# Half of the attention weights transposed by DMA as float16 pairs instead of by TensorE, and two feed-forward stages exchanged

## The chip, the cores and the metric

One core of one Trainium2 chip. The metric is the device time of one execution in microseconds, the median of the runs shown. Float32 in, float32 out.

## The reference

Three computations in a row. Sizes: batch 2, 8 heads, 576 positions, head width 64, so 1152 tokens of 512 features.

```python
scores = (q @ k.T) / 8                          # 576 x 576 per batch and head
kth    = the 32nd largest score of each row
attn   = softmax over the scores >= kth; all other weights 0
x = (attn @ v), heads side by side              # 1152 x 512
h = x @ w_in                                    # 512 -> 2048
y = (max(h, 0) + alpha * min(h, 0)) @ w_out     # 2048 -> 512
out = ((y @ w_a) * (y @ w_b)) @ w2              # 512 -> 1536 -> 512
```

## The kernel before

**Tiles and groups.** Attention is cut into 72 tiles: 128 query rows of one head (kind `T`), or 64 rows of two heads (kind `L`, the last 64 positions). `M1` (L46) sorts the tiles into six groups of output tokens, which the two feed-forward layers then take as their columns. Groups 0 and 1 are 128 tokens of batch 0 (8 tiles each), group 2 is 256 tokens of batch 0 (16 tiles), group 3 is 256 tokens: the last 64 of batch 0, the last 64 and the first 128 of batch 1 (16 tiles), group 4 is 256 tokens of batch 1 (16 tiles), group 5 is 128 tokens of batch 1 (8 tiles).

**One attention tile.** `front` (L406): TensorE makes the scores, ScalarE copies them to SBUF. `middle` (L419): VectorE finds the 32 largest of each row with four MAX8 and three MATCH_REPLACE8 (L424 to L433), ScalarE takes the exponential (L437), VectorE masks it and sums (L440), GpSimd scales the rows (L444). `back` (L450), for the tile before: TensorE turns the 128 x 576 weights round in five float32 transposes (L458, L460), ScalarE copies the two PSUM tiles to the tile `pt` (L459, L461). `av` (L466), after the last tile of a unit (one `L` tile, two heads of one `T` tile, or two heads of two neighbouring `T` tiles): ten float32 matmuls (twenty instructions, in two column halves of TensorE, L481) multiply with `v`; ScalarE and VectorE write the result to `xT` as a float16 high and low part (L488, L489). `fetch_v` loads `v` again for each group and head pair (28 loads).

**The feed-forward layers.** `moe1(g)` and `moe2(g)` are the first and second layer for the tokens of group g. From group 2 on both run in float16 pairs: each value is a high and a low part and three matmuls stand for one (`contract` L550, `project` L562). The high part is a cast on ScalarE (L540), the low part a subtraction on GpSimd (L541). `finish` (L615) turns the result of `moe1` round for `moe2`: a square with its sum (L620), power-of-two scales on VectorE (L109 to L111), two casts (L630, L631), eight transposes (L635), a copy (L636).

**What sets the order.** `ORDER` (L48) lists the stages: (1, 4) is `moe1` of group 4. Three tracks are interleaved by a planner's clocks (L739 to L867): `dve_track` (conversion of the weights, then attention, 6.1 planned us a tile, given out in ninths, `STEPS`), `mlp_track` (the stages), `bg_track` (weights rewritten as float16 pairs). A stage `moe1(g)` waits until the attention of group g is planned to be done. The framework then gives every engine a fixed order of its own, in which it runs without overtaking. All loads and the stores of rewritten weights are issued by SP, in one order too: `q` and `k` (L328, L347), `v` (L339), the weight blocks of the last layer (L246, L251, L672). Outputs go out from ScalarE's queue.

Of the kernel before, what the change touches and what calls it, by code (L numbers as in the profile page):

```python
# [8 lines left out]
F32 = mybir.dt.float32  # L9
F32R = mybir.dt.float32r  # L10
F16 = mybir.dt.float16
# [5 lines left out]
AF = mybir.ActivationFunctionType  # L17
ALU = mybir.AluOpType

P = 128  # L20
B, H, S, D = 2, 8, 576, 64
# [6 lines left out]
HALF = S // 2  # L28
NEG = -3.0e38

NORM = "pool"
RLOB = 3
W2B = 3
# [2 lines left out]
VB = 2  # L36
# [4 lines left out]
PB = 3  # L41
# [6 lines left out]
ORDER = ((1, 0), (2, 0), (1, 1), (2, 1), (1, 2), (2, 2), (1, 3), (2, 3), (1, 4), (1, 5), (2, 4), (2, 5))  # L48
# [14 lines left out]
KBACK = 2  # L63
# [17 lines left out]
def tile_topk_attention_moe(ctx: ExitStack, tc: tile.TileContext, qT, kT, vM, vL, wi, wo, al, wa, wb, w2, out):  # L81
    nc = tc.nc
    cp = ctx.enter_context(tc.tile_pool(name="cp", bufs=1))
    sp = ctx.enter_context(tc.tile_pool(name="sp", bufs=2))
# [48 lines left out]
    vsc = small("vsc", 2)  # L133
# [181 lines left out]
    late = []  # L315
# [6 lines left out]
    qcur, xts = {}, {}  # L322
    kcur, vcur = {}, {}
# [43 lines left out]
    for g, grp in enumerate(M1):  # L367
        cols_of = {}
        col = 0
        for kind, b, t in grp:  # L370
            cols_of[kind, b, t] = col
            col += P if kind == "T" else D
        for hp in range(4):

            units = []
            for kind, b, t in grp:
                if units and len(units[-1]) < 2 and kind == "T" and units[-1][0][:2] == (kind, b):
                    units[-1].append((kind, b, t))
                else:
                    units.append([(kind, b, t)])  # L380
            for unit in units:
                pts_of = {}
                for slot, (kind, b, t) in enumerate(unit):
                    n = P if kind == "T" else D
                    heads = [[2 * hp], [2 * hp + 1]] if kind == "T" else [[2 * hp, 2 * hp + 1]]
                    for i, hs in enumerate(heads):
                        tiles.append(dict(g=g, b=b, t=t if kind == "T" else 4, hp=hp, hs=hs, n=n, col=cols_of[unit[0]], slot=slot,
                                          wide=len(unit) * P, pts=pts_of, last=slot == len(unit) - 1 and i == len(heads) - 1))
        gsize.append(col)

    def fetch(tl):
        b, t, hp = tl["b"], tl["t"], tl["hp"]
        tl["k"] = {h: get_k(b, h) for h in tl["hs"]}
        if (b, t, hp) not in qcur:
            qcur[b, t, hp] = prep_q(b, t, hp)

    def fetch_v(tl):
        b, t, hp = tl["b"], tl["t"], tl["hp"]
        if (tl["g"], b, hp) not in vcur:
# [19 lines left out]
    def middle(tl, s):  # L419
        m8 = sp.tile([P, 32], F32, tag="m8", name="m8", bufs=3)  # L420
        nb = sp.tile([P, 1], F32, tag="nb", name="nb", bufs=2)
        e = sp.tile([P, S], F32, tag="e", name="e", bufs=EB)
        wk = sp.tile([P, S], F32, tag="wk", name="wk", bufs=WKB)
        nc.vector.max(m8[:, 0:8], s)  # L424
        nc.gpsimd.tensor_scalar(nb, m8[:, 0:1], -0.125, None, op0=ALU.mult)
        yield 1
        src = s
        w2 = lambda t: t.rearrange("p (a n) -> p a n", a=2)
        ep = None
        for r in range(1, 4):  # L430
# [10 lines left out]
        nc.vector.tensor_scalar(sm[:, 1:2], sm[:, 0:1], 1e-9, None, op0=ALU.add)  # L441
# [5 lines left out]
        tl["e"] = e  # L447
        yield 1

    def back(tl):  # L450
        e = tl["e"]
        j = tl["hs"][0] % 2
        if tl["slot"] == 0:
            tl["pts"][j] = sp.tile([P, 5, 2 * P], F32, tag="pt", name="pt", bufs=PB)
        pt = tl["pts"][j][:, :, tl["slot"] * P:tl["slot"] * P + P]
# [10 lines left out]
    def av(pair_):  # L466
        tl = pair_[-1]
        g, hp, n, col = tl["g"], tl["hp"], tl["n"], tl["col"]
        v = vcur[g, tl["b"], hp]
        if g not in xts:  # L470
            if split_in[g] or gsize[g] > P:
                xts[g] = late[0].tile([P, 4, 256], F32, tag="xT", name=f"xT{g}", bufs=XB)
            else:
                xts[g] = sp.tile([P, 4, P], F32, tag="xe", name=f"xe{g}", bufs=2)
        o = psum("o", "T")
        wd = tl["wide"]
        for c in range(5):
            for j in range(2):
                pt = tl["pts"][j if n == P else 0]
                pt = pt[:, c, 0:wd] if n == P else pt[:, c, j * D:(j + 1) * D]  # L480
                nc.tensor.matmul(o[j * D:(j + 1) * D, 0:n if n == D else wd], v[:, c, j * D:(j + 1) * D], pt, start=c == 0, stop=c == 4)  # L481
        if n == P:
            n = wd
        for r, c in [(slice(0, P), slice(0, n))]:
            if split_in[g]:
                x = split_view(xts[g])
                xh = x[r, 0, hp, col:col + n]
                nc.scalar.activation(xh, o[r, c], AF.Copy, scale=vsc[r, 0:1])  # L488
                nc.vector.scalar_tensor_tensor(x[r, 1, hp, col:col + n], o[r, c], vsc[r, 0:1], xh, op0=ALU.mult, op1=ALU.subtract)  # L489
            else:  # L490
                nc.scalar.activation(xts[g][r, hp, col:col + n], o[r, c], AF.Copy)

    def attention():
        for tl in tiles[0:F0]:
            fetch(tl)
        ready = [front(tiles[0])]
        yield ("begin", 0)
        for tl in tiles[F0:FA]:
            fetch(tl)
        ready += [front(tl) for tl in tiles[1:QA]]  # L500
        for tl in tiles[0:VA]:
            fetch_v(tl)
        prev = None
        pr = []
        for i, tl in enumerate(tiles):
            s = ready.pop(0)
            for k, _ in enumerate(middle(tl, s)):
                if k == 0 and i + FA < len(tiles):
                    fetch(tiles[i + FA])
                if k == 1 and i + VA < len(tiles):  # L510
                    fetch_v(tiles[i + VA])
                if k == KBACK and prev is not None:
                    back(prev)
                    pr.append(prev)
                    if prev["last"]:
                        av(pr)
                        pr = []
                    yield ("done", prev["g"])
# [6 lines left out]
        av(pr)  # L525
        yield ("done", prev["g"])


    def wide(tag, bufs):
# [226 lines left out]
    def dve_track():  # L756
        att = attention()
        cnt = [0] * len(M1)
# [10 lines left out]
        def advance():  # L769
            r = next(att, None)  # L770
            if isinstance(r, tuple):
                cnt[r[1]] += 1
                if cnt[r[1]] == need[r[1]]:
                    att_done[r[1]] = clock["dve"] + 3
                return 1
            return r and 0

        for kind, k, *more in DVE:
# [5 lines left out]
            if kind == "mix":  # L784

                done, steps = 0, 0
# [16 lines left out]
            else:  # L803
                left = k
                while left:
                    r = advance()
# [103 lines left out]
```

## Time and profile before

| what | us |
|---|---|
| three runs | 724.32, 725.1, 728.9 |
| median | 725.1 |
| profiled execution | 727.69 |
| its span, first to last instruction | 725.9 |
| TensorE busy in the span | 634.6 (87%) |
| VectorE | 570.8 (79%) |
| ScalarE | 471.4 (65%) |
| GpSimd | 377.3 (52%) |

The profiled execution lies 2.6 us above the median, and 1.8 us of it lie outside the span. Times in the rows below count from the span's first instruction. PE is TensorE, PEld its weight loads, DVE VectorE, ACT ScalarE, POOL GpSimd, SPq the issuing queue of SP. A matmul's listed duration is longer than the distance to the next one, since matmuls are pipelined.

### The profile page before, as it was taken

The page shows a single profiled execution, that of the slowest core. Times are in us where ns is not written, and L with a number is a line of the kernel's source. Part 1 is how long each engine was busy: PE and PEld are TensorE (multiplying, and loading weights), DVE is VectorE, ACT ScalarE, POOL GpSimd, SP SyncE. Part 2 cuts the span into 40 slices and gives each one's busy share as a digit, 9 for nine tenths or more (in the row PEclk, how much of TensorE's full clock was granted, in tenths as well). Part 3 has the DMA queues.
Part 4 walks back from the last instruction along what each step waited for, and adds up shares of the span by engine and source line. Part 5 has one row for each costly group of instructions (what it writes and reads, how often), then busy time and mean ns, then how long its engine had stood idle before and what let it go on. Part 6 is the DMA issues. An engine that isn't in the chain of part 4 may idle for free.

```text
span 725.9 us, 14586 instructions
## 1 busy us (share of the span) xinstructions
PE 634.6 (87%) x5002; PEld 473.2 (65%) x5002; DVE 570.8 (79%) x1462; ACT 471.4 (65%) x995; POOL 377.3 (52%) x540
## 2 busy tenths in 40 slices
PE   1456866999979889799869999999999999999997
PEld 1334655687756658567637877766777777677775
DVE  3999899789989998998579799999889899322121
ACT  4878987896789877888676544556445455543222
POOL 5776788886655666879564422433223233221111
PEclk9975569999999999899989999999999999999999
DMA  6976999994411133212545134010122300002243
GB/s 176 326 248 198 352 290 288 311 339 130 133 43 28 26 93 87 76 52 85 163 142 156 54 83 121 28 32 22 26 67 80 98 17 17 2 2 59 61 129 102
DMA packets 60410, 86.15 MB, mean 119 GB/s; under 512 B 7984, under 2 KB 34608, under 8 KB 60336
## 3 DMA queue, kind: packets, MB, share of 16 engines
q1 hardware_dynamic: 59024, 82.87, 36.7%
q10 hardware_dynamic: 1312, 2.36, 0.9%
q8 instruction: 39, 0.64, 0.4%
q14 instruction: 35, 0.29, 0.1%
HBM read 76.55 MB, written 8.65 MB: 117 GB/s over the span
## 4 chain that ended last, share of the span: by engine, by line
PE 47%; DVE 3%; ACT 3%; DMA 2%; issue 2%; POOL 1%; POOLq 0%; ACTq 0%; DVEq 0%
PE h L550 8%; PE y L562 8%; PE ha L550 8%; PE hb L550 8%; PE o L562 7%; PE o L481 3%; PE ps L413 3%; DMA w2s<-w_st 2%; PE t L458 2%; DVE m L433 1%; DVE wk L431 1%; ACT xT L636 1%; PE t L460 0%; ACT wsc L248 0%; DVE e L440 0%
## 5 line engine op out<-in xcount | busy, mean ns | idle before, releaser
L433 DVE MAX8 m<-wk 128x8 f32<-128x576 f32 x216 | 162.8, 754 | 2.0
L541 POOL TENSOR_TENSOR gp<-gt,gp 128x256 f16<-128x256 f32 (+1 forms) x112 | 68.2, 610 | 150.9 <-ACT gp L540 141.6
L431 DVE MATCH_REPLACE8 wk<-m,wk 128x576 f32<-128x576 f32 x144 | 106.8, 742 | 0.0
L550 PE MATMUL h<-xT,wi_sb 128*128 128x256 f16 (+1 forms) x960 | 100.1, 251 | 5.1 <-DVE gp_n L599 4.0
L550 PEld LDWEIGHTS <-wi_sb 128*128 128x128 f16 x960 | 79.1, 98 | 27.1 <-issue 11.0
L540 ACT ACTIVATE gp<-gt 128x256 f16<-128x256 f32 (+1 forms) x112 | 43.4, 388 | 74.6 <-DVE gt L690 52.6
L562 PEld LDWEIGHTS <-gp 128*128 128x128 f16 x588 | 54.9, 98 | 47.0 <-ACT gp L540 1.9
L562 PE MATMUL y<-wo_sb,gp 128*128 128x512 f16 x336 | 84.1, 379 | 0.6 <-ACT gp L540 0.4
L444 POOL TENSOR_SCALAR e<-e,sm 128x576 f32<-128x576 f32 x72 | 55.1, 765 | 51.0 <-DVE sm L442 44.5
L413 PE MATMUL ps<-ks,qh 128*128 128x288 f32 x160 | 49.9, 390 | 32.2 <-DVE e L440 23.1
L424 DVE MAX8 m<-s 128x8 f32<-128x576 f32 x72 | 54.2, 753 | 26.7 <-ACT s L416 25.1
L690 DVE SCALAR_TENSOR_TENSOR gt<-hb,wb_inv,r 128x256 f32<-128x256 f32 (+1 forms) x48 | 21.4, 446 | 61.2 <-PE hb L550 59.7
L550 PE MATMUL ha<-xT,wa_sb 128*128 128x256 f16 (+1 forms) x576 | 65.7, 262 | 1.6 <-ACT xT L636 1.6
L550 PE MATMUL hb<-xT,wb_sb 128*128 128x256 f16 (+1 forms) x576 | 64.3, 260 | 0.0
L562 PE MATMUL o<-w2s,gp 128*128 128x512 f16 x252 | 63.6, 380 | 0.4 <-ACT gp L540 0.2
L481 PE MATMUL o<-pt,v 128*64 128x128 f32 (+2 forms) x640 | 56.8, 319 | 5.4 <-ACT pt L459 2.3
L550 PEld LDWEIGHTS <-wa_sb 128*128 128x128 f16 x576 | 51.1, 99 | 15.6 <-issue 2.6
L440 DVE SCALAR_TENSOR_TENSOR e<-s,m,ep 128x576 f32<-128x576 f32 x72 | 58.0, 806 | 2.3 <-ACT ep L437 0.2
L413 PEld LDWEIGHTS ps<-ks,qh 128*128 128x128 f32 x160 | 29.1, 214 | 43.9 <-issue 14.9
L190 ACT ACTIVATE rlo<-raw 128x512 int16<-128x512 uint32 x68 | 53.8, 791 | 5.7 <-DMA raw<-in_wi_dram 3.9
L458 PE MATMUL t<-ident,e 128*128 128x128 f32 x288 | 48.1, 293 | 10.5 <-POOL e L444 10.3
L437 ACT ACTIVATE ep<-s,nb 128x576 f32<-128x576 f32 x72 | 53.7, 745 | 3.0 <-POOL ql L353 0.6
(192 smaller groups left out, 1411.6 us busy)
## 6 DMA issues: line engine op xcount, KB each, us to landing
w2s<-w_pr SPq DMA_DIRECT2D x48, 256.0 KB, 2.6
w2s<-w_st SPq DMA_DIRECT2D x36, 256.0 KB, 2.7
raw<-in_wi_dram SPq DMA_DIRECT2D x16, 512.0 KB, 6.3
raw<-in_wo_dram SPq DMA_DIRECT2D x16, 512.0 KB, 6.7
v<-in_vM_dram SPq DMA_DIRECT2D x28, 256.0 KB, 3.2
raw<-in_wa_dram SPq DMA_DIRECT2D x12, 512.0 KB, 5.3
raw<-in_wb_dram SPq DMA_DIRECT2D x12, 512.0 KB, 5.1
raw<-in_w_dram SPq DMA_DIRECT2D x12, 512.0 KB, 5.4
```

The costliest lines, as they stand in the source:

```text
L190: nc.scalar.activation(r.bitcast(I16).rearrange("p (n t) -> p n t", t=2)[:, :, 0], lo, AF.Copy, scale=2.0 ** -29)
L413: nc.tensor.matmul(ps[:, f, 0:HALF], q[:, h % 2, :], ks[h][:, f * HALF:(f + 1) * HALF], start=i == 0, stop=i == len(mm) - 1)
L424: nc.vector.max(m8[:, 0:8], s)
L431: nc.vector.match_replace(out=wk, in_to_replace=m8[:, 8 * r - 8:8 * r], in_values=src, imm_value=NEG)
L433: nc.vector.max(m8[:, 8 * r:8 * r + 8], wk)
L440: nc.vector.scalar_tensor_tensor(w2(e), w2(s), m8[:, 31:32], ep, op0=ALU.is_ge, op1=ALU.mult, accum_out=sm[:, 0:1])
L444: nc.gpsimd.tensor_scalar(e, e, sm[:, 1:2], 1.0, op0=ALU.mult, op1=ALU.mult)
L458: nc.tensor.transpose(t1[:, c * P:(c + 1) * P], e[:, c * P:(c + 1) * P], ident)
L481: nc.tensor.matmul(o[j * D:(j + 1) * D, 0:n if n == D else wd], v[:, c, j * D:(j + 1) * D], pt, start=c == 0, stop=c == 4)
L541: nc.gpsimd.tensor_sub(l[:, 0:n], t[:, 0:n], h[:, 0:n])
L550: nc.tensor.matmul(dst[:, 0:n], w[a][:, c * P:(c + 1) * P], x[:, b, c, 0:n], start=k == 0, stop=k == 11)
L562: nc.tensor.matmul(dst, act[b][:, s], w[a], start=i == 0 and k == 0, stop=i == last and k == 2)
```

## The change

For tiles of batch 1 (the second half, tiles 36 to 71) `back` no longer uses TensorE. The scaled weights, times 2^14, are cast to float16 on ScalarE, the remainder is made by two subtractions on GpSimd, both halves stand side by side in `e16` (128 x 1152, one buffer), and one transposing DMA from SP writes nine 128 x 128 blocks into `pt`. `v` of batch 1 is loaded once per head pair, at tiles 20, 26, 38 and 40, and kept as a float16 pair (`v_pair`). `av` multiplies high by high, low by high and high by low: 28 float16 matmuls instead of 20 float32 instructions, and it stands one tile later (`KAV`). In group 3 the four `L` tiles of batch 0 come first. In `ORDER`, `moe2` of group 4 comes ahead of `moe1` of group 5. A "done" step now covers a whole unit instead of a tile, so a tile takes between 8.25 and 8.5 planner steps instead of nine. The tile `xe` has one buffer instead of two.

```diff
-ORDER = (..., (1, 4), (1, 5), (2, 4), (2, 5))
+ORDER = (..., (1, 4), (2, 4), (1, 5), (2, 5))
+KLIFT = 3
+KAV = 1
+KV = 4
+V_AT = {20: 0, 26: 1, 38: 2, 40: 3}
...
+    def v_pair(hp):
...
+        raw = flat(sp.tile([P, 5, 2 * P], F32, tag="pt", name="vraw", bufs=PB))...
+        nc.sync.dma_start(raw[:, 0:4, :], vM[1, :, :, c0:c0 + 2 * D])
+        for r in (slice(0, D), slice(D, P)):
+            nc.sync.dma_start(raw[r, 4, :], vL[1, :, c0:c0 + 2 * D])
+        vh, vl = pr[:, 0:5], pr[:, 5:10]
+        nc.scalar.activation(flat(raw), flat(raw), AF.Copy, scale=vsc[:, 0:1])
+        nc.scalar.activation(flat(vh), flat(raw), AF.Copy)
+        nc.gpsimd.tensor_sub(flat(vl), flat(raw), flat(vh))
+        nc.gpsimd.memset(vl[D:P, 4], 0.0)
...
+        if tl["lift"]:      # in middle, after the scaling on GpSimd
+            e16 = late[0].tile([P, 2 * S], F16, tag="e16", name="e16", bufs=1)
+            nc.scalar.activation(e16[:, 0:S], e, AF.Copy)
+            nc.gpsimd.tensor_sub(e16[:, S:S + D], e[:, 512:S], e16[:, 512:S])
+            nc.gpsimd.tensor_sub(e16[:, S + D:2 * S], e[:, 0:512], e16[:, 0:512])
...
+        if tl["lift"]:      # in back
+            pt = lifted(tl["pts"][j])[:, :, tl["slot"] * P:tl["slot"] * P + P]
+            nc.sync.dma_start_transpose(pt, e)
+            return
...
+        if lift:            # in av
+            ops = [(vh, c, c) for c in range(5)] + [(vh, c, 5 + c) for c in range(4)] + [(vl, c, c) for c in range(5)]
+            for i, (w, a, c) in enumerate(ops):
+                for j in range(2):
...
+                    nc.tensor.matmul(o[j * D:(j + 1) * D, ...], w[:, a, j * D:(j + 1) * D], pt, start=i == 0, stop=i == 13)
...
+                if k == KV and i in V_AT:
+                    v_pair(V_AT[i])
+                if k == KAV and due:
+                    p = due.pop(0)
+                    av(p)
+                    yield ("done", p[0]["g"], len(p))
```

## Rows read from the trace of the kernel before

**Rows 1.** The page: busy tenths of the engines in 40 equal slices.

```profile
PE   1456866999979889799869999999999999999997
...
DVE  3999899789989998998579799999889899322121
```

**Rows 2.** Stretches: us, busy (instructions) of PE, PEld, DVE, ACT, POOL; clock, DMA share, GB/s.

```profile
293.00:387.00 94.00, 77.45 (x576) 54.46 (x574) 74.95 (x186) 74.02 (x151) 67.77 (x103) 0.91 0.36 110
...
511.00:572.00 61.00, 61.00 (x468) 46.59 (x468) 53.96 (x126) 28.34 (x61) 18.31 (x33) 0.97 0.22 63
572.00:626.00 54.00, 54.00 (x429) 38.93 (x427) 44.76 (x109) 27.62 (x64) 18.54 (x33) 1.00 0.11 32
626.00:726.00 100.00, 94.96 (x950) 71.67 (x948) 22.56 (x62) 35.42 (x93) 19.98 (x40) 1.00 0.22 64
```

**Rows 3.** VectorE alone: stretch, us, busy (instructions), clock, DMA share, GB/s.

```profile
387.00:557.00 170.00, 155.83 (x374) 0.99 0.21 62
557.00:615.00 58.00, 55.25 (x131) 1.00 0.16 47
```

**Rows 4.** VectorE's groups between 437 and 557 us (one masking instruction per tile).

```profile
L440 DVE SCALAR_TENSOR_TENSOR e<-s,m,ep 128x576 f32<-128x576 f32 x16 | 13.0, 810 | 1.0
```

**Rows 5.** The chain that ended last, pieces of it: start us, us, what.

```profile
565.39 2.31 PE o L481 x20
...
578.46 0.44 PE t L458 x4
578.89 0.11 PE t L460
...
579.65 1.31 PE h L550 x12
...
581.39 1.24 PE o L481 x20
...
702.76 0.67 PE ha L550 x12
```

**Rows 6.** Groups of ScalarE and GpSimd: busy us, mean ns, idle before.

```profile
L459 ACT ACTIVATE pt<-t 128x512 f32<-128x512 f32 x72 | 42.8, 595 | 18.0 <-PE t L458 17.4
L461 ACT ACTIVATE pt<-t 128x128 f32<-128x128 f32 x72 | 20.0, 277 | 3.2 <-PE t L460 3.2
L250 POOL TENSOR_TENSOR w2s<-wsc,w2s 128x512 f16<-128x512 f32 x12 | 13.9, 1158 | 11.4 <-ACT w2s L249 8.7 <-issue 1.8 <-POOL w2s L250 0.8
L331 ACT ACTIVATE ks<-kr 128x576 fp32r<-128x576 f32 x16 | 10.8, 676 | 3.3 <-DMA kr<-in_kT_dram 2.0 <-PE ps L413 1.3
L361 POOL TENSOR_TENSOR ql<-qr,qh 128x64 fp32r<-128x64 f32 x16 | 4.8, 321 | 0.0
```

**Rows 7.** DMA issues: KB each, median us from issue to landing.

```profile
w2s<-w_pr SPq DMA_DIRECT2D x48, 256.0 KB, 2.6
...
raw<-in_wo_dram SPq DMA_DIRECT2D x16, 512.0 KB, 6.7
...
qr<-in_qT_dram SPq DMA_DIRECT2D x64, 64.0 KB, 2.3
...
alpha<-in_al_dram SPq DMA_DIRECT2D x1, 8.0 KB, 1.6
```

**Rows 8.** What SP's queue waited for: us in total, times, longest.

```profile
SPq L672 <- PE o L562: 166.8, 43, 59.3
...
SPq L339 <- PE o L481: 50.0, 12, 15.1
```

**Rows 9.** Timeline at the end of `moe1` of groups 3 and 5.

```profile
501.99 1.46 PE L562 MATMUL y<-wo_sb,gp 128*128 128x512 f16 x6
...
510.99 1.22 PE L550 MATMUL ha<-xT,wa_sb 128*128 128x256 f16 x5 [1.58 <-ACT xT L636]
...
652.05 0.59 PE L562 MATMUL y<-wo_sb,gp 128*128 128x512 f16 x2
...
657.85 1.02 ACT L636 ACTIVATE xT<-tp 128x1024 f16<-128x1024 f16 x1
```

More of the change, by code (lines that the diff above doesn't have):

```diff
@@ L29 @@
 NEG = -3.0e38
+LIFT = 2.0 ** 14
+KLIFT = 3
+KAV = 1
+KV = 4
+V_AT = {20: 0, 26: 1, 38: 2, 40: 3}
 NORM = "pool"
@@ L46 @@
 M1 = [[('T', 0, 0)], [('T', 0, 1)], [('T', 0, 2), ('T', 0, 3)], [('L', 0, 0), ('L', 1, 0), ('T', 1, 0)], [('T', 1, 1), ('T', 1, 2)], [('T', 1, 3)]]
[L48 removed]
+ORDER = ((1, 0), (2, 0), (1, 1), (2, 1), (1, 2), (2, 2), (1, 3), (2, 3), (1, 4), (2, 4), (1, 5), (2, 5))
 PAIRS = ("wi", "wo", "wa", "wb", "w2")
@@ L372, in tile_topk_attention_moe @@
             col += P if kind == "T" else D
-        for hp in range(4):
+        lead = grp[0][0] == "L" and len(grp) > 1
+        for part, hp in [(p, h) for p in ((grp[:1], grp[1:]) if lead else (grp,)) for h in range(4)]:
             units = []
-            for kind, b, t in grp:
+            for kind, b, t in part:
                 if units and len(units[-1]) < 2 and kind == "T" and units[-1][0][:2] == (kind, b):
@@ L387, in tile_topk_attention_moe @@
                         tiles.append(dict(g=g, b=b, t=t if kind == "T" else 4, hp=hp, hs=hs, n=n, col=cols_of[unit[0]], slot=slot,
-                                          wide=len(unit) * P, pts=pts_of, last=slot == len(unit) - 1 and i == len(heads) - 1))
+                                          wide=len(unit) * P, pts=pts_of, lift=b == 1, last=slot == len(unit) - 1 and i == len(heads) - 1))
         gsize.append(col)
@@ L395, in fetch @@
             qcur[b, t, hp] = prep_q(b, t, hp)
+    vpair = {}
+    def v_pair(hp):
+        c0 = hp * 2 * D
+        flat = lambda t: t.rearrange("p c n -> p (c n)")
+        if hp < 2:
+            pr = late[0].tile([P, 5, 2 * D], F32, tag="vp", name=f"vp{hp}", bufs=2)
+        else:
+            pr = sp.tile([P, 5, 2 * D], F32, tag="v", name=f"vp{hp}", bufs=VB)
+        pr = flat(pr).bitcast(F16).rearrange("p (c n) -> p c n", c=10)
+        raw = flat(sp.tile([P, 5, 2 * P], F32, tag="pt", name="vraw", bufs=PB))[:, 0:5 * P].rearrange("p (c n) -> p c n", c=5)
+        nc.sync.dma_start(raw[:, 0:4, :], vM[1, :, :, c0:c0 + 2 * D])
[6 more added lines that the diff above has]
+        nc.gpsimd.memset(vl[D:P, 4], 0.0)
+        vpair[hp] = vh, vl
     def fetch_v(tl):
         b, t, hp = tl["b"], tl["t"], tl["hp"]
-        if (tl["g"], b, hp) not in vcur:
+        if not tl["lift"] and (tl["g"], b, hp) not in vcur:
             v = sp.tile([P, 5, 2 * D], F32, tag="v", name=f"v{b}{t}{hp}", bufs=VB)
@@ L440, in middle @@
         nc.vector.scalar_tensor_tensor(w2(e), w2(s), m8[:, 31:32], ep, op0=ALU.is_ge, op1=ALU.mult, accum_out=sm[:, 0:1])
-        nc.vector.tensor_scalar(sm[:, 1:2], sm[:, 0:1], 1e-9, None, op0=ALU.add)
+        if tl["lift"]:
+            nc.vector.tensor_scalar(sm[:, 1:2], sm[:, 0:1], 1e-9, 1.0 / LIFT, op0=ALU.add, op1=ALU.mult)
+        else:
+            nc.vector.tensor_scalar(sm[:, 1:2], sm[:, 0:1], 1e-9, None, op0=ALU.add)
         nc.vector.reciprocal(sm[:, 1:2], sm[:, 1:2])
@@ L447, in middle, with lifted @@
         tl["e"] = e
+        if tl["lift"]:
[3 more added lines that the diff above has]
+            nc.gpsimd.tensor_sub(e16[:, S + D:2 * S], e[:, 0:512], e16[:, 0:512])
+            tl["e"] = e16
         yield 1
+    def lifted(t):
+        return t.rearrange("p c n -> p (c n)").bitcast(F16)[:, 0:9 * 2 * P].rearrange("p (c n) -> p c n", c=9)
     def back(tl):
@@ L468, in av @@
         g, hp, n, col = tl["g"], tl["hp"], tl["n"], tl["col"]
-        v = vcur[g, tl["b"], hp]
+        lift = tl["lift"]
+        if lift:
+            vh, vl = vpair[hp]
+        else:
+            v = vcur[g, tl["b"], hp]
         if g not in xts:
@@ L473, in av @@
             else:
-                xts[g] = sp.tile([P, 4, P], F32, tag="xe", name=f"xe{g}", bufs=2)
+                xts[g] = sp.tile([P, 4, P], F32, tag="xe", name=f"xe{g}", bufs=1)
         o = psum("o", "T")
         wd = tl["wide"]
-        for c in range(5):
+        if lift:
+            ops = [(vh, c, c) for c in range(5)] + [(vh, c, 5 + c) for c in range(4)] + [(vl, c, c) for c in range(5)]
+            for i, (w, a, c) in enumerate(ops):
+                for j in range(2):
+                    pt = lifted(tl["pts"][j if n == P else 0])
+                    pt = pt[:, c, 0:wd] if n == P else pt[:, c, j * D:(j + 1) * D]
+                    nc.tensor.matmul(o[j * D:(j + 1) * D, 0:n if n == D else wd], w[:, a, j * D:(j + 1) * D], pt, start=i == 0, stop=i == 13)
+        for c in range(0 if lift else 5):
             for j in range(2):
@@ L503, in attention @@
         prev = None
-        pr = []
+        pr, due = [], []
         for i, tl in enumerate(tiles):
@@ L511, in attention @@
                     fetch_v(tiles[i + VA])
-                if k == KBACK and prev is not None:
+                if k == KV and i in V_AT:
[4 more added lines that the diff above has]
+                    yield ("done", p[0]["g"], len(p))
+                if prev is not None and k == (KLIFT if prev["lift"] else KBACK):
                     back(prev)
                     pr.append(prev)
-                    if prev["last"]:
+                    if prev["last"] and prev["lift"]:
+                        due.append(pr)
+                        pr = []
+                    elif prev["last"]:
                         av(pr)
+                        yield ("done", prev["g"], len(pr))
                         pr = []
-                    yield ("done", prev["g"])
                 if k == KFRONT and i + QA < len(tiles):
@@ L524, in attention @@
         pr.append(prev)
-        av(pr)
-        yield ("done", prev["g"])
+        for p in due + [pr]:
+            av(p)
+            yield ("done", p[0]["g"], len(p))
     def wide(tag, bufs):
@@ L771, in advance @@
             if isinstance(r, tuple):
-                cnt[r[1]] += 1
+                cnt[r[1]] += r[2]
                 if cnt[r[1]] == need[r[1]]:
                     att_done[r[1]] = clock["dve"] + 3
-                return 1
+                return r[2]
             return r and 0
```

6 lines of the change are left out of this document (4 added, 2 removed).

## The prediction

> **What bounds the kernel now.** I read the page's forty slices first [rows 1]. TensorE stands at eight or nine tenths from the sixth slice on, VectorE at the same height up to slice 34, where the last attention tile ends, and at two or three tenths behind it. So two engines are nearly full side by side for most of the kernel, and TensorE alone at its end. The stretches make that exact [rows 2]. From 511 to 572 us (`moe2` of group 3 beside the attention of group 4) TensorE is busy all 61 us; from 572 to 626 (`moe1` of group 4 beside the attention of group 5) all 54 us; from 626 on 95 of 100. Only 293 to 387 us is different: there TensorE leaves 16.5 us and VectorE 19 us of 94 unused, while ScalarE (74) and GpSimd (68) rewrite weights and loads through SP's queue stand between them. VectorE alone [rows 3] is busy 155.8 us of the 170 from 387 to 557, so 14.2 us are idle, and 55.3 of 58 behind that. That decides how a saving on TensorE is to be counted: ahead of 572 us, where `moe1` of group 4 waits for the attention of group 4, it is worth no more than VectorE's idle time; behind 572 us it is worth all of itself.
>
> **TensorE's saving.** In the chain the five transposes of a tile cost 0.44 + 0.11 = 0.55 us [rows 5]. All 36 tiles of batch 1 lose them: 19.8 us. The product with `v` goes from 20 instructions to 28. A float16 matmul of 256 columns costs 1.31 / 12 = 0.109 us, one of 128 columns 0.67 / 12 = 0.056 us [rows 5]. A float32 transpose of 128 columns costs 0.11 us, twice the float16 price; twenty float32 instructions of 256 columns would cost 20 x 0.22 = 4.4 us at that rate, and the row has 2.31 us. So the two column halves run side by side already, and I take the same for the new 14 pairs: 14 x 0.109 = 1.53 us instead of 2.31 for a unit of four tiles (0.8 saved, four units in group 4), 14 x 0.056 = 0.78 instead of 1.24 for a unit of two (0.46 saved, four in group 3, four in group 5). That is 3.1 + 3.7 = 6.8 us. If the halves did not overlap in float16, the units would cost 3.05 and 1.57 us and the product would lose 5.6 us instead; I take the overlapped value and keep the other for the range. Split by stretch: ahead of 572 us 28 x 0.55 + 3.1 + 1.8 = 20.3 us, behind it 8 x 0.55 + 1.8 = 6.2 us.
>
> **Ahead of 572 us.** Of the 20 us only VectorE's gaps can be cashed in: 14.2 us between 387 and 557, and part of the 19 us before 387. VectorE's instructions per tile stay as they were. I count 11 of the 14.2, because some gaps are waits for scores and exponentials from ScalarE that remain, and 2 of the earlier 19, since there the new casts, subtractions and transposes of tiles 36 to 40 and the two late loads of `v` meet the engines and the queue that are busy already. Together 13 us. The bounds are 0 (VectorE keeps its pace) and about 25.
>
> **What the other engines get.** ScalarE loses 0.595 + 0.277 us of copies per tile and gains one cast of 128 x 576, for which a cast of that size in another place has 0.676 us [rows 6]: 0.2 us less. GpSimd gains two subtractions per tile; the nearest rows are 0.321 us (64 columns) and 1.158 us (512 columns) [rows 6], so 1.5 us a tile and 53 us in all. Between 511 and 572 us it is busy 18.3 of 61 us [rows 2], and some eight tiles a stretch add 12: it has room. The four `v` pairs cost by the same rows about 1.5 us on ScalarE and as much on GpSimd each, beside a full TensorE; the 12 loads of `v` that go are off the path, but SP's queue waited 50 us for TensorE to free `v` buffers [rows 8], with loads of `q` and of weights behind it. I cost this at nothing either way.
>
> **The transposing DMA.** The trace has none, so its time to landing, L, is bounded. It moves 288 KB. A 64 KB load lands after 2.3 us, a 256 KB one after 2.6, a 512 KB one, at a busy time, after 6.7 [rows 7]. The nearest is the 256 KB row; scaled it gives 2.9 us, and I take 3.5, since a turned block is not a plain row. What it may cost is set by the single buffer `e16`: the cast for the next tile waits on ScalarE until the DMA has read the last one, and behind that cast stand the next exponential and score copy, for which VectorE waits. One turn of that ring is the cast 0.68, the subtractions 0.32 and 1.16, some 0.7 us queued behind other work of GpSimd (my estimate, one subtraction's order) and L: 2.86 + L. The attention has one tile per 120 / 16 = 7.5 us [rows 4]. So L = 3.5 gives a ring of 6.4 us, hidden; at L = 4.6 us it is as slow as the tiles are now, and each further us of L costs 36 us. On SP the transpose also waits for GpSimd, and loads of `q` and of `w2` queue behind it, for a us or two; the queue itself is mostly waiting for TensorE to free weight buffers (166.8 us [rows 8]), so the loads come ahead of need. For the product with `v` the landing has about one whole tile, which 3.5 us fits. The Trainium skill speaks to L twice, and not with one voice. "VectorE: DVE Perf Modes", section "The three transpose paths", gives the DMA 1309 ns for one 128 x 128 block against 390 ns on TensorE; nine of them one after another would be 11.8 us, and the time by it some 250 us above the time before. "DMA: Bandwidth & Descriptors", section "Latency and other measured facts", gives 261 GB/s for such DMAs, which is 1.1 us of moving for 288 KB, inside what I take. No row here shows either.
>
> **The exchanged stages.** Before, the end of `moe1` of groups 4 and 5 was covered by the start of the next independent stage. Now `moe2` of the same group follows at once and needs the turned result. In group 5's case, from the last matmul (652.05 + 0.59) to the copy's end (657.85 + 1.02) it took 6.2 us [rows 9], then with other work in its way; I count 5 us of idle TensorE for it. In group 4's case the nearest is group 3, 503.45 to 510.99 us [rows 9], 7.5 us in which attention filled most and the last 1.6 us were a plain wait; I count 2. What the exchange buys is that TensorE need not wait for the attention of group 5, which VectorE finishes no sooner than about 64 us after that of group 4 (eight tiles at 7 us and the way through the DMA), while `moe1` of group 4 with a lighter attention takes some 50. That wait does not stand in the time before, so it is a loss avoided and no gain.
>
> **Sum.** -13 ahead of 572, -6.2 behind it, +7 for the two uncovered ends: -12.2 us on the profiled 727.7, 715.5. The median lies 2.6 us under the profiled execution, so **713 us**.
>
> **Rivals.** (A, slower) The ring of `e16` becomes the bound: at L = 4.6 us the 13 us ahead of 572 are gone, the rest (-6.2 + 7) leaves 726, and from there (L - 4.6) x 36 us are added: 748 at 5.2, 802 at 6.7 (the 512 KB row). For it: one buffer, four engines in the ring. Against it: the rows of half that size. (B, no change) VectorE keeps its pace: 3 us instead of 13, so 723. For it: 55.3 of 58 us busy [rows 3]. (C, more) VectorE's gaps close altogether and 8 of the 19 us before 387 go, because SP no longer stands still for `v`: -22 - 6.2 + 7, 704; with the uncovered ends filled as well, 699. (D, slower) The nine blocks of a transpose go one after another, each at the price of the smallest DMA, 1.6 us [rows 7]: L = 14.4, a ring of 17.3 us, 9.8 x 36 = 350 us more, 1076. The first of the two rules above points this way.
>
> **How the numbers follow.** Forecast 0.42, A 0.17, B 0.22, C 0.14, D 0.05. About 1% is what a measurement of this kernel tells from no change, so faster ends at 717.9 and slower begins at 732.4. The forecast lies mostly under the first bound (0.37), C wholly, B now and then: faster 0.53. B and the rest of the forecast make the same 0.25, A and D slower 0.22. The range goes from C's far end, with a little under it, to A at L = 5.0: 696 to 742; outside are D and most of A. It also holds the case that the column halves don't overlap, +12 us of TensorE's time of which some 4 lie behind 572.
>
> **What will show it.** Right: L near 3.5 us; VectorE over 95% busy from 400 us to the end of attention; no wait of ScalarE's cast for the DMA; TensorE idle for about 5 us just before the last `moe2`. Wrong: a cast that waits for the transpose in most tiles and a tile every 8 us or more (A, D), or attention of group 4 that ends where it did, with TensorE idle instead (B). A wait of the product with `v` for its DMA would put the miss on the one tile of slack.

## The result, and the profile after

The change makes the kernel slightly slower: 729.8 us (median of 20 runs) against 725.0 (20 runs), a ratio of 1.0054, 95% interval 1.0032 to 1.0076. One of before's 20 took 3489 us; it does not touch the median, and the ratio leaves it out. The forecast was 713, 12 us under the kernel before. The profiled execution after took 729.4 us, its span 727.6: by the profiled executions the change costs 1.7 us, by the medians 4.8.

TensorE's busy time did fall, from 634.6 to 617.7 us, and GpSimd's busy time rose from 377.3 to 429.9, by the 53 us that were forecast. The stretches of after, in the columns of [rows 2, 3], show what became of TensorE's saving:

```profile
293.00:387.00 94.00, 75.72 (x581) 51.98 (x579) 82.88 (x202) 74.98 (x154) 76.03 (x123) 0.91 0.40 108
387.00:557.00 170.00, 161.18 (x1329) 119.61 (x1329) 157.31 (x382) 94.20 (x186) 94.96 (x151) 0.96 0.44 104
...
557.00:615.00 58.00, 56.18 (x467) 39.52 (x467) 54.01 (x128) 30.67 (x64) 31.20 (x50) 1.00 0.35 70
572.00:626.00 54.00, 49.07 (x423) 33.48 (x422) 41.99 (x107) 27.68 (x57) 24.55 (x40) 1.00 0.29 54
626.00:726.90 100.90, 93.78 (x912) 70.67 (x909) 19.28 (x49) 31.30 (x83) 19.98 (x40) 0.96 0.22 64
```

VectorE was to close its gaps between 387 and 557 us. It is busy 157.3 us there instead of 155.8 [rows 3], so its pace hardly moves. Its last masking instruction of group 4 ends at 553.3 us (556.6 before), of group 5 at 612.3 (615.4). TensorE is now idle for 5 of the 54 us from 572 to 626, where it was full [rows 2], and its clock, the column before the last two, is 0.96 instead of 0.99 or 1.00 in two of the rows.

The new operations themselves cost what the forecast gave them. First the DMA's row (issues, median us to landing) [rows 7], then ScalarE's cast, GpSimd's two subtractions and VectorE's masking between 437 and 557 us, as in [rows 4, 6]:

```profile
pt<-e SPq DMA_TRANSPOSE x36, 3.3
```

```profile
L479 ACT ACTIVATE e<-e 128x576 f16<-128x576 f32 x36 | 24.5, 681 | 20.0 <-POOL e L473 15.4 <-DMA pt<-e 3.6 <-POOL ql L366 0.6
...
L481 POOL TENSOR_TENSOR e<-e,e 128x512 f16<-128x512 f32 x36 | 41.8, 1160 | 0.0
L480 POOL TENSOR_TENSOR e<-e,e 128x64 f16<-128x64 f32 x36 | 11.1, 308 | 16.9 <-ACT e L479 15.6 <-PE ps L439 0.8
...
L466 DVE SCALAR_TENSOR_TENSOR e<-s,m,ep 128x576 f32<-128x576 f32 x16 | 12.9, 808 | 0.6
```

The transpose lands after 3.3 us (3.5 taken); the cast waits for it 3.6 us in all 36 tiles. `moe1` of group 4 starts at 566.2 us instead of 571.9, 5.7 earlier where 13 were forecast, and from there to TensorE's last matmul it takes 157.5 us instead of 150.1, 7.4 longer where 0.8 were forecast (+7 for the ends, -6.2). The two misses are 7.3 and 6.6 us.

The two exchanged stages appear as forecast. The timeline of after at the end of `moe1` of group 4, and at that of group 5, against [rows 9]:

```profile
616.03 2.33 PE L626 MATMUL y<-wo_sb,gp 128*128 128x512 f16 x10
...
620.05 0.94 PE L529 MATMUL o<-pt,vp 128*64 128x128 f16 x27 [1.69 <-DMA pt<-e]
...
623.58 1.47 PE L614 MATMUL ha<-xT,wa_sb 128*128 128x256 f16 x12 [1.28 <-ACT xT L700]
...
689.69 2.59 PE L626 MATMUL y<-wo_sb,gp 128*128 128x512 f16 x9
...
694.22 0.40 PE L699 MATMUL tp<-ident,yb 128*128 128x128 f16 x4 [1.94 <-ACT yb L694]
695.00 0.61 PE L699 MATMUL tp<-ident,yb 128*128 128x128 f16 x4 [0.39 <-DVE yb L695]
695.65 1.02 ACT L700 ACTIVATE xT<-tp 128x1024 f16<-128x1024 f16 x1 [1.49 <-PE tp L699]
696.72 1.44 PE L614 MATMUL ha<-xT,wa_sb 128*128 128x128 f16 x12 [1.11 <-ACT xT L700]
```

Between the last `y` matmul (689.69 + 2.59) and the first `ha` lie 4.4 us with 1.0 us of transposes in them, and TensorE comes out of it at half clock, 0.50 in this stretch:

```profile
695.00:700.00 5.00, 3.88 (x36) 3.73 (x37) 0.35 (x1) 1.43 (x3) 0.00 (x0) 0.50 0.02 3
```

### The profile page after: what moved, and what is told of

It is laid out like the page before. It is cut to its first block, busy times and chain, and to the rows that moved or that the text cites. A ratio compares the mean times of both kernels' runs of the same rounds, so it can differ in the third digit from the quotient of the medians.

```text
span 727.6 us, 14588 instructions
## 1 busy us (share of the span) xinstructions
PE 617.7 (85%) x4950; PEld 456.9 (63%) x4950; DVE 574.8 (79%) x1462; ACT 471.9 (65%) x967; POOL 429.9 (59%) x608
## 4 chain that ended last, share of the span: by engine, by line
PE 50%; DVE 17%; ACT 9%; DMA 8%; issue 5%; POOL 4%; SPq 1%; POOLq 0%; ACTq 0%; DVEq 0%
PE h L614 7%; PE hb L614 6%; PE ha L614 6%; PE o L626 6%; PE y L626 6%; DVE wk L457 4%; DVE m L459 4%; PE ps L439 3%; DMA pt<-e 3%; PE hb L618 2%; PE o L534 2%; DMA w2s<-w_st 2%; PE ha L618 2%; PE o L629 2%; DVE e L466 2%
## 5 line engine op out<-in xcount | busy, mean ns | idle before, releaser
L614 PE MATMUL h<-xT,wi_sb 128*128 128x256 f16 (+1 forms) x960 | 97.3, 251 | 1.5 <-DVE gp_n L663 0.7
L614 PEld LDWEIGHTS <-wb_sb 128*128 128x128 f16 x576 | 51.5, 100 | 6.9 <-issue 0.7
L442 ACT ACTIVATE s<-ps 128x576 f32<-128x576 f32 x72 | 46.5, 646 | 12.9 <-PE ps L439 12.5
```

The costliest lines, as they stand in the source:

```text
L442: nc.scalar.activation(s.rearrange("p (a n) -> p a n", a=2), ps[:, :, 0:HALF], AF.Copy)
L614: nc.tensor.matmul(dst[:, 0:n], w[a][:, c * P:(c + 1) * P], x[:, b, c, 0:n], start=k == 0, stop=k == 11)
```

## The experiments

Ratios are to the kernel before, run beside each of them on the same chip; its median there was 726.8 to 727.9 us.

**The exchange and the planner's steps.** Five kernels take the change apart: without the exchange (e1), without the shorter tiles of the planner (e2), the exchange alone (e3), the steps alone (e5), and what is left without exchange and shorter tiles: the DMA, the `v` pairs and the order within group 3 (e6, "DMA alone").

```diff
 e1: after, e3: before, each with the other's ORDER
-ORDER = (..., (1, 4), (2, 4), (1, 5), (2, 5))   # e3: the reverse
+ORDER = (..., (1, 4), (1, 5), (2, 4), (2, 5))
 e2: after; e6: e1 (the steps go back to nine a tile)
+                    else:
+                        yield 1
 e5: before, "done" once a unit
...
+                        yield ("done", prev["g"], len(pr))
-                    yield ("done", prev["g"])
```

> The changed kernel with the old ORDER (moe1 of group 5 ahead of moe2 of group 4 again). Theory U (uncovered ends): the exchange leaves TensorE idle for 4.3 us after moe1 of group 4 and 4.4 us after moe1 of group 5, and some 3 us more go to the half clock behind the second gap; with the old order these 12 us go, and a wait of about 3 us for the attention of group 5 comes (done at 621 us, moe1 of group 4 at 618): about 9 us less than the changed kernel, 720 to 722 us. Theory P (planner): the miss is in batch 0, where stages start 2.6 to 4.8 us late; the old order then changes nothing, 729 to 731, or costs a wait. Theory D (the DMA is late): as P, 728 to 731.

> The changed kernel with nine planner steps per tile again (a plain step wherever a tile is turned round without ending its unit). Theory P: batch 0's stages start where they did before, 4 to 5 us earlier than in the changed kernel: 725. Theory U and theory D: the steps do nothing for the end, 729 to 731.

> The kernel before with nothing but the new ORDER. Theory U: there the attention of group 5 is done at 626 us, just when moe1 of group 4 ends, so the exchange avoids no wait and only costs the two uncovered ends: 10 to 12 us more than before, 735 to 737. Theories P and D: no change of over 2 us, 723 to 727.

> The kernel before with the unit-wise done step alone (8.25 to 8.5 planner steps a tile instead of nine), nothing turned by DMA, old order. In the changed kernel the shorter steps were worth 9 us (739.2 with nine against 729.8). Theory S (they let VectorE's attention run ahead of the feed-forward work, with or without the DMA): 4 to 9 us less than before, 716 to 721. Theory L (they only matter where tiles are turned by DMA and a landing is needed): within 2 us of before, 723 to 728.

> The changed kernel with the old order and nine steps, so the turning by DMA and the kept v pairs alone. If the parts add up: 739.2 less the 7.3 us that the old order gave, 732, so the turning by DMA costs 5 to 7 us by itself although TensorE has 17 us less to do. Theory V (VectorE is the bound ahead of the last two groups, the DMA's way costs nothing): 720 to 725.

| kernel | us | ratio, 95% interval |
|---|---|---|
| e1, after in the old order | 722.5 | 0.9948, 0.9918 to 0.9978 |
| e2, after with nine steps | 739.2 | 1.0179, 1.0146 to 1.0212 |
| e3, exchange alone | 738.4 | 1.0166, 1.0130 to 1.0202 |
| e5, steps alone | 745.2 | 1.0266, 1.0221 to 1.0311 |
| e6, DMA alone | 729.7 | 1.0062, 1.0026 to 1.0097 |

The exchange costs 11.5 us on the kernel before (738.4 less 726.9) and 7.3 us on after (729.8 less 722.5, two runs apart in time; by their ratios 1.1%). The timeline of e3 shows the same uncovered end as after:

```profile
701.07 2.59 PE L562 MATMUL y<-wo_sb,gp 128*128 128x512 f16 x9
705.60 0.40 PE L635 MATMUL tp<-ident,yb 128*128 128x128 f16 x4 [1.94 <-ACT yb L630]
...
708.11 1.12 PE L550 MATMUL ha<-xT,wa_sb 128*128 128x128 f16 x9 [1.11 <-ACT xT L636]
```

The steps, which the prediction never priced, count twice over. Alone they cost 18 us (e5), which none of the expectations had (716 to 728 us); with the DMA they gain 1.1% (e6 to e1), which no expectation for e2 had (725 to 731 us). In the profiles that gain lies in `moe1` of group 2, which takes 107.6 us in e6 and 96.5 in e1 (94.3 in before), and e6 makes up a part of it later; why the steps matter there stayed open. Of the loss in e5, 14 us lie in `moe1` of group 3 (74.2 us instead of 60.1), and the timeline shows why. With fewer steps a tile, more attention falls on the end of `moe1` of group 3, and there TensorE's queue holds transposes that wait for GpSimd, and scores behind them that wait for a buffer that VectorE frees:

```profile
518.99 1.12 PE L458 MATMUL t<-ident,e 128*128 128x128 f32 x4 [3.47 <-POOL e L444]
...
525.13 1.11 PE L458 MATMUL t<-ident,e 128*128 128x128 f32 x4 [1.11 <-POOL e L444]
...
529.01 0.85 PE L413 MATMUL ps<-ks,qh 128*128 128x288 f32 x2 [1.08 <-DVE e L440]
...
530.14 2.41 PE L550 MATMUL ha<-xT,wa_sb 128*128 128x256 f16 x12
```

From the last `y` matmul (512.2) to the first `ha` pass 18 us; before it was 7.5 [rows 9]. With the transposes on SP's queue those waits no longer stand in TensorE's.

So e1 keeps everything that was to bring the gain and leaves out what costs. It gains 0.5%: 4.4 us by the medians, and in the profile 2.7 us ahead of `moe1` of group 4 (569.2 against 571.9) and 0.8 behind it (149.3 us to the last matmul against 150.1). The forecast had 19 us for these two. The rest of the study asks where they went.

**The DMA's ring.** e4 issues the transpose of after twice.

```diff
             nc.sync.dma_start_transpose(pt, e)
+            nc.sync.dma_start_transpose(pt, e)
```

> The changed kernel with each transposing DMA issued twice, one after the other, into the same place. The landing is 3.3 us now, so about 6.6 us for both. Theory D (the DMA's way already holds up the product with v and the cast): each added us shows in most of the 36 tiles, +80 to +120 us. My prediction's ring (2.86 us + L against 7.3 us a tile): 9.5 us a tile, +79 us. Theory U with a ring that has more slack than I counted: under +20 us.

797.2 us, 1.0969 (1.0916 to 1.1023). The second one is issued when the first has landed, 3.2 us later, and the next cast starts when the second has (timeline of e4), so this is a ring with 3.3 us more of landing. The waits of its stretch from 391 to 640 us (us, times, longest) show the two places that the prediction named:

```profile
530.26 1.26 SPq L495 DMA_TRANSPOSE pt<-e  x1
533.48 1.30 SPq L496 DMA_TRANSPOSE pt<-e  x1
...
536.77 0.68 ACT L479 ACTIVATE e<-e 128x576 f16<-128x576 f32 x1 [2.40 <-DMA pt<-e]
```

```profile
ACT e L479 <- DMA pt<-e: 104.8, 28, 5.8
PE o L530 <- DMA pt<-e: 35.2, 15, 8.6
```

It costs 67 us over after (797.2 less 729.8), 1.9 us a tile for 36 tiles. So on average 1.4 of the 3.3 us were slack; the prediction had 1.1 us of slack at L = 3.5. The ring is not what bounds after.

**VectorE.** The prediction counted a saving ahead of 572 us only as far as VectorE has gaps. e7 (before) and e8 (e1) leave out the fourth search round in batch 1.

```diff
-        for r in range(1, 4):
+        rounds = 3 if tl["b"] else 4
+        for r in range(1, rounds):
...
+        for _ in range(2 * (4 - rounds)):
+            yield 1
```

> The kernel before without the fourth round of the search in batch 1 (one MATCH_REPLACE8 and one MAX8 left out of 36 tiles, so 24 weights a row are kept): VectorE has 1.5 us less per tile, 57 us in all. TensorE is full in most of that time, so both theories expect little: 4 to 10 us less than before, 715 to 721.

> The changed kernel with the old order, also without the fourth round in batch 1. Theory V (TensorE's saving is there and only VectorE's pace hides it): with VectorE relieved the saving shows, 15 to 20 us below the same cut in the kernel before, 697 to 705. Theory R (the way through cast, subtractions and DMA, 2.2 us and 3.3 us and queues in one buffer, is the next bound at 6 to 7 us a tile): no more than 5 us below it, 712 to 720.

e7: 728.1 us, 1.0034 (0.9995 to 1.0073). e8: 722.3 us, 0.9951 (0.9914 to 0.9988), the same as e1. Every expectation was lower (715 to 721 for e7, 697 to 720 for e8): the shorter search gains nothing in either kernel. VectorE's row of [rows 3] in e8:

```profile
387.00:557.00 170.00, 160.04 (x1300) 117.08 (x1301) 132.66 (x332) 94.20 (x188) 96.92 (x154) 0.95 0.45 103
```

VectorE has 37 us idle there instead of 16 in e1, and the attention of group 4 ends at 541.8 us instead of 556.1 in e1. Still `moe1` of group 4 starts at 570.1 (569.2 in e1). VectorE's pace alone did not hold e1 back.

**Where TensorE's saving went.** Two stretches with the same feed-forward work can be compared: from the first matmul of `moe2` of group 2 to that of `moe1` of group 4, and from there to the first matmul of the last `moe2`. Before:

```profile
387.80:571.90 184.10, 181.11 (x1444) 135.99 (x1443) 167.59 (x401) 96.08 (x212) 62.63 (x115) 0.99 0.21 62
571.90:648.60 76.70, 76.02 (x681) 55.05 (x680) 52.89 (x137) 41.95 (x103) 25.04 (x48) 1.00 0.08 23
```

e1, with the stretch of its half clock:

```profile
392.10:569.20 177.10, 169.78 (x1366) 125.07 (x1366) 161.09 (x387) 93.98 (x186) 94.97 (x151) 0.95 0.43 98
569.20:645.00 75.80, 72.55 (x677) 50.64 (x676) 52.95 (x137) 41.07 (x96) 34.58 (x60) 1.00 0.24 46
...
504.30:518.00 13.70, 10.63 (x68) 8.56 (x67) 10.06 (x28) 5.63 (x9) 3.08 (x5) 0.50 0.20 37
```

In the first stretch busy time times clock is 179.3 us before and 161.3 in e1: TensorE has 18.0 us less to do. The stretch is 7.0 us shorter. The rest went into waits: TensorE is idle for 7.3 us instead of 3.0, and the missing part of the clock takes 8.5 us instead of 1.8. In the second stretch TensorE is busy 3.5 us less, and of that 0.9 us shows and 2.6 us are idle; its longest waits there are the product's for its DMA, 2.1 us. And e1 enters the first stretch late: `moe2` of group 2 starts at 392.1 us, 4.3 behind before's 387.8. Of these, 2.2 us are a longer `moe1` of group 2, the stage of the first turned tiles (96.5 us against 94.3; after has 96.4, e3 and e11, both without the DMA, 94.4 and 94.5); the other 2.1 us come before it, where before and e11, which run the same work up to there, differ by 4.9 us.

The largest single loss in e1 lies at the end of `moe1` of group 3. Before (timeline, then the stretch from the last `y` matmul to the first `ha`):

```profile
503.38 2.38 PE L481 MATMUL o<-pt,v 128*64 128x256 f32 x20
...
506.32 0.60 PE L458 MATMUL t<-ident,e 128*128 128x128 f32 x4
...
508.36 1.05 PE L635 MATMUL tp<-ident,yb 128*128 128x128 f16 x16
```

```profile
503.45:510.99 7.54, 4.85 (x45) 3.35 (x46) 7.44 (x25) 6.40 (x13) 1.16 (x3) 1.00 0.14 41
```

e1:

```profile
499.87 1.47 PE L626 MATMUL y<-wo_sb,gp 128*128 128x512 f16 x6
...
503.38 0.40 PE L699 MATMUL tp<-ident,yb 128*128 128x128 f16 x4 [2.04 <-ACT yb L694]
...
505.93 3.15 PE L529 MATMUL o<-pt,vp 128*64 128x256 f16 x27 [1.57 <-DMA pt<-e]
...
510.01 1.01 PE L699 MATMUL tp<-ident,yb 128*128 128x128 f16 x8 [0.39 <-DVE xT L543]
...
512.13 2.72 PE L614 MATMUL ha<-xT,wa_sb 128*128 128x256 f16 x12 [1.11 <-ACT xT L700]
```

```profile
501.34:512.13 10.79, 5.68 (x47) 4.86 (x48) 9.88 (x30) 6.64 (x12) 3.59 (x6) 0.64 0.32 65
```

TensorE is idle for 5.1 us of 10.8 in e1, for 2.7 of 7.5 before. Of attention's own transposes only one tile's five stood here before, 0.9 us by their listed durations. More of the difference is the product with `v`: before it ran at once, while ScalarE and VectorE prepared `y`; in e1 it waits 1.6 us for its DMA, stands between the two halves of `y`'s transposes and runs at half clock. How long the clock stays down differs even between executions of the same work: after, whose order differs from e1's only behind `moe1` of group 4, has the half clock from 503.6 for 6.8 us, e1 from 504.3 for 13.7. So after takes 173.6 us for the first of the two stretches, e1 177.1. The stretch of e1's half clock, in after:

```profile
504.30:518.00 13.70, 11.17 (x96) 9.55 (x96) 12.75 (x32) 8.43 (x14) 5.58 (x9) 0.78 0.21 41
```

Three small edits tried to fill or shorten this end: matmuls whose result nobody reads, after the last `y` matmul (nine) and after the transposes (five), in groups 2 and 3 (e10; e11 is the control on before); the product with `v` two planner steps later (e9); the layer's end ahead of attention's steps (e12); later e9 and e12 together (e15).

```diff
 e10 (e1), e11 (before), at two places
+                if g in (2, 3) and t == nt - 1:
+                    dm = psum("dm")
+                    for _ in range(5):
+                        nc.tensor.matmul(dm, yl[:, 0:P], halves("wo", NF1 - 1)[0], start=True, stop=True)
 e9, e15
-KAV = 1
+KAV = 3
 e12, e15
-HPY = 0
+HPY = 100
```

> The changed kernel with the old order and the product with v two planner steps later (KAV = 3). Theory G (TensorE's saving is lost in gaps: between 391 and 572 us it has 160 us of own work by counts and prices in 181 us, 12 us of the rest in gaps of over 0.15 us, some 9 us in half clock): the waits of the product for its DMA, 6 us in all the attention, go, 2 to 4 us less than with the old order alone, 718 to 721. Theory W (every wait is only moved to what comes next): 722 to 724.

> The changed kernel with the old order, and 14 matmuls of 512 columns whose result nothing reads, put on TensorE at the end of moe1 of groups 2 and 3: nine behind the last matmul of the layer, five behind the eight transposes. Theory G: they keep the clock up where nothing is left to do; the half clock behind 504 us (13.7 us long, so 6.8 us of work) shortens to 3 to 7 us, and the time falls by 2 to 5 us, 717 to 720. Theory W: they only stand in the way, 723 to 728.

> The kernel before with the same 14 matmuls. There attention's own transposes fill that end, and the half clock is 3.4 us long. Theory G: no gain, 0 to 4 us more than before, 725 to 729. Theory W: 725 to 729 as well; were this one faster too, the half clock would cost the kernel before as much and would not explain where the saving went.

> The changed kernel with the old order and the turning of y for the second layer put ahead of everything ready at that time (HPY = 100). With the old order a product with v that waits 1.6 us for its DMA stands between the transposes of group 3's y. Theory G: the end of moe1 of group 3 (10.8 us from its last matmul to the first of moe2, 7.6 us in the kernel before) gets back to 8 or 9 us, 2 to 3 us less, 719 to 721. Theory W: 722 to 725.

> The kernel of e1 with both small edits of e9 and e12: weights' products three steps later, and the first layer's end ahead of attention's steps. If the two gains are real and add up: 719 to 721 us, 0.990 of before. If both are the scatter of a new fixed order: 720 to 726 us.

| kernel | us | ratio, 95% interval |
|---|---|---|
| e9 | 722.3 | 0.9932, 0.9903 to 0.9960 |
| e10 | 725.3 | 0.9967, 0.9943 to 0.9991 |
| e11 | 729.7 | 1.0028, 1.0000 to 1.0055 |
| e12 | 721.7 | 0.9932, 0.9904 to 0.9959 |
| e15 | 724.5 | 0.9970, 0.9942 to 0.9997 |

The four on e1 are not told apart from it (0.9918 to 0.9978), the two small gains don't add up, and e11 gains nothing on before. The end itself, 10.8 us in e1, took 9.8 us in e9, 7.7 in e10, 11.7 in e12 (so that edit did not shorten it) and 8.5 in e15. e10 is instructive. Its end is as short as before's, and its stretches show the clock full where it was halved (0.76 to 0.84 in this stretch in e9 and e12), yet it gains nothing; idle time and half clock come later:

```profile
499.00:520.00 21.00, 17.98 (x143) 12.27 (x142) 20.66 (x58) 12.91 (x24) 10.07 (x16) 1.00 0.27 54
569.00:640.00 71.00, 66.87 (x593) 45.89 (x592) 50.52 (x129) 36.81 (x84) 31.55 (x53) 0.95 0.21 44
```

**Opening the ends, and both bounds.** So the end of group 3 alone does not set the time. e13 and e14 take away what makes TensorE wait there and in group 2: the second layer of groups 2 and 3 reads the attention result instead of `y`. e16 and e17 do that and leave out the fourth search round as well.

```diff
 e13 (e1), e14 (before); e16 = e13 and e17 = e14 with the edit of e7
-                nc.scalar.activation(split_view(xts[g])[:, :, :, o0:o0 + P], tp, AF.Copy)
+                if g in (2, 3):
+                    nc.scalar.activation(yb.rearrange("p (a c n) -> p a c n", a=2, c=4), tp, AF.Copy)
+                else:
+                    nc.scalar.activation(split_view(xts[g])[:, :, :, o0:o0 + P], tp, AF.Copy)
```

> This kernel is that of e1 with the last copy of a first layer's end (groups 2 and 3) no longer what the second layer reads: moe2 of groups 2 and 3 reads the attention result instead of y, so it needn't wait for the layer's end. Left out: that dependence, nothing of the work. Theory G (the 12 us of TensorE's own work that the change saves between 391 and 572 us are lost at the layer ends, in waits and half clock): 706 to 712 us, 10 us or more under e1, while the same cut in the kernel before gains only 4 to 8 us. Theory W (the waits move elsewhere in the fixed order, whatever end is opened): e13 is 0 to 5 us under e1, and stays about 4 us under e14.

> The kernel before with the same cut: moe2 of groups 2 and 3 reads the attention result instead of y, so that it needn't wait for the end of the first layer. Theory G: 717 to 721 us, since its ends were filled by attention's own transposes, and the distance to e13 grows from 4 to about 10 us. Theory W: 4 us over e13, whatever both gain.

> The kernel of e13 (open layer ends of groups 2 and 3) whose search takes three rounds instead of four in batch 1. Left out: the last round of the search there, so that 24 weights of a row are kept in place of 32, and the dependence of moe2 of groups 2 and 3 on y. Theory F (two bounds one behind the other: first the layer ends, and when those are open VectorE's attention, on which TensorE of e13 waits for some 9 us more behind 555 us than e14): with both gone TensorE's saving shows, 705 to 711 us, and e16 is 6 us or more under e17. Theory W (the fixed order loses it wherever it is opened): 715 to 720 us, as e13, and within 3 us of e17.

> The kernel of e14 (the kernel before with open layer ends of groups 2 and 3) with three rounds of the search in batch 1. Left out: the same as in e16. TensorE has 2.5 us of gaps left behind 555 us in e14, so both theories expect little: 715 to 719 us. They differ in its distance to e16: 6 us or more by theory F, within 3 us by theory W.

| | transposes on TensorE | by DMA, old order | difference |
|---|---|---|---|
| as it is | 1 | 0.9948 (e1) | -0.5% |
| search shorter | 1.0034 (e7) | 0.9951 (e8) | -0.8% |
| ends open | 0.9881 (e14) | 0.9875 (e13) | -0.1% |
| both | 0.9824 (e17) | 0.9700 (e16) | -1.2% |

The intervals of the last two rows: 0.9844 to 0.9907 (e13, 718.9 us), 0.9847 to 0.9916 (e14, 718.4), 0.9662 to 0.9739 (e16, 704.8), 0.9786 to 0.9863 (e17, 713.6). With the ends open both kernels gain, before 8.7 us by the ratios and e1 5.3, so the ends cost time in the old kernel too. But the distance between them does not grow to 10 us, as theory G had it; it goes to nothing. Theory W's constant 4 us did not hold either. The stretches of e14 and then of e13 show where e13 loses it:

```profile
560.00:610.00 50.00, 49.42 (x383) 35.83 (x382) 46.54 (x111) 27.97 (x62) 17.69 (x32) 1.00 0.12 35
610.00:645.00 35.00, 34.15 (x355) 25.01 (x354) 11.00 (x36) 18.92 (x51) 8.19 (x18) 1.00 0.01 1
```

```profile
560.00:610.00 50.00, 47.21 (x396) 32.75 (x397) 49.13 (x119) 28.06 (x57) 26.95 (x43) 1.00 0.26 56
610.00:645.00 35.00, 30.01 (x308) 22.24 (x307) 9.30 (x33) 16.51 (x44) 9.64 (x20) 0.85 0.10 19
```

```profile
618.32 1.65 PE L529 MATMUL o<-pt,vp 128*64 128x128 f16 x27 [1.32 <-DMA pt<-e]
```

TensorE of e13 reaches `moe1` of group 5 at 610.7 us, but the last product with `v` that it needs (the third fence, timeline of e13) is made at 618.3. Between 560 and 645 us TensorE is idle for 7.8 us (1.4 in e14), and then at a clock of 0.85. So behind the layer ends stands the attention's pace: the shorter search, worth nothing in e8, is worth 14 us here (e13 to e16; 4.8 from e14 to e17). Theory F had foretold 6 us or more between e16 and e17: with both gone part of TensorE's saving shows, 8.8 us. That is clear of the third row's distance; from the second row's (5.8 us, e7 to e8) it is not told apart. TensorE of e16 is full where e13 waited:

```profile
610.00:645.00 35.00, 35.00 (x332) 26.08 (x330) 8.04 (x22) 15.04 (x38) 8.06 (x17) 1.00 0.09 24
```

The 8.8 us are still less than half of the 18.0 + 3.5 us by which TensorE's work fell in e1. Part of the rest stands in the stretch from 390 to 450 us, where TensorE of e17 (first) is busy 4.3 us longer than that of e16, which is idle instead; what would close that stayed open.

```profile
390.00:450.00 60.00, 58.20 (x512) 44.50 (x510) 48.31 (x116) 32.42 (x73) 23.45 (x45) 1.00 0.34 100
```

```profile
390.00:450.00 60.00, 53.94 (x497) 39.73 (x497) 43.75 (x108) 32.12 (x66) 36.25 (x56) 0.99 0.60 153
```

## Why the prediction was wrong

- **The saving on TensorE** was right in kind and size: 18.0 us less work between `moe2` of group 2 and `moe1` of group 4 in e1, where 24 of the 28 tiles fall for which 20.3 was forecast. The transposes are gone, and the float16 halves run side by side (27 matmuls of a two-tile unit in 0.94 us at 620.05, 0.78 forecast for 28).
- **"Ahead of 572 us ... 13 us" is the step that failed.** It took VectorE for the only thing that could keep TensorE from cashing in its saving. e8 has 22 us less of VectorE's work there than e1, and the time did not move. Measured: 2.7 us (e1) in place of 13. Where 11 us were to come behind 387 us, 7.0 did; the other 11.0 of the 18.0 went into TensorE's idle time (4.3) and its half clock (6.7), which had no term in the sum. Where 2 us were to come ahead of 387, `moe2` of group 2 starts 4.3 later, 2.2 of it gathered in `moe1` of group 2. What holds TensorE is not one wait. Shortening the end of group 3 does nothing (e10), opening the ends gains as much or more in the old kernel (e13, e14), and the saving shows best when the ends are open and VectorE has less to do. Which wait of the fixed order takes which part of the 11 us was not shown.
- **"Behind 572 us it is worth all of itself" failed too.** 0.8 us in e1 in place of 6.2: TensorE's busy time falls by 3.5 us in `moe1` of groups 4 and 5, and 2.6 of that come back as idle time. TensorE at nine tenths in [rows 2] does not say that the work taken off it comes off the time.
- **VectorE as a limit** was half right: in the kernel with the DMA it is a bound once the layer ends are open (14 us, e13 to e16), and none as long as they are closed (e1 to e8). Rival B had a time, 723, that e1 meets (722.5), and its signs came: the attention of group 4 ends at 556.1 us (556.6 before) with TensorE idle instead. But its reason falls with e8, so the time was met by luck.
- **The exchange** was sized right, +7 us for +7.3 measured, but the "loss avoided" that was to pay for it did not exist. I had let the attention of group 5 begin with `moe1` of group 4. It begins when VectorE is done with group 4, at 553.3 us in after, 13 us ahead of that stage. So the last masking instruction is over at 612.3, `moe1` of group 4 at 618.4, and the last product with `v` follows at 620. There was next to nothing to wait for in the old order, and e1 has 7.3 us less.
- **The planner's steps** were not priced at all. They cost 18 us on the kernel before and gain some 8 with the DMA.
- **The DMA** was right: 3.3 us to landing for 3.5, no wait of the cast in most tiles, slack 1.4 us for 1.1. Rivals A and D fall. The Trainium skill's price in "VectorE: DVE Perf Modes", section "The three transpose paths", would give an estimate of 11.8 us if nine blocks were paid one by one; the trace has 3.3 for all nine, so the blocks of one transfer are not added up here.
- **Two slips without weight.** Rival C's "699" should be 697 (704 less the 7 us of both ends). And "attention filled most" of group 3's end: TensorE was busy 4.85 of 7.54 us there, about 1 us of it with `y`'s own transposes, so attention filled about half.

Of the signs that were to show it, L, the cast's wait and the idle time ahead of the last `moe2` came as the forecast had them. The one that decides, VectorE over 95% busy, did not: 157.3 of 170 us is 93%, against 92% before.

## What to carry to other kernels

A busy engine is not yet a bound: before work is taken off it, ask for every stage what else would have to be earlier for the stage to end earlier. Here TensorE lost 18 us of work in a stretch that became 7 us shorter; the rest turned into waits. A test of one edit can hide a bound behind another: the shorter search was worth nothing with closed layer ends and 14 us with open ones, which only the four corners (each bound open or not, in the old and the new kernel) showed. Price every edit of the schedule, the planner's step counts and the order of stages too: here they moved the time by more (-8 to +18 us) than the work they came with.

## What was not expected of the hardware

TensorE's clock more than doubled the price of the waits: between the same two stage starts idle time grew by 4.3 us from before to e1, and the clock took 6.7 us more. After the end of `moe1` of group 3 in e1, with 3.3 of the 5.3 us before 504.3 busy, the granted clock was 0.50 (1.2 GHz) for 13.7 us, up to 518.0; in after, with the same instructions, for 6.8 us; in the kernel before, for 3.4 us, from 511.0. Spare matmuls took that stretch away (e10) and one of 6.8 us came at 574.5, where the clock had been full in e1. And the transposing DMA kept its 3.2 us to landing when twice as many ran, one behind the other (e4), with SP's queue held for 1.3 us an issue.
